# Rounding the expert activation to its high part: all 96 on ScalarE instead of 28 there and 68 on VectorE

## The chip, the cores and the metric

The kernel runs on one core of a Trainium2 chip. The metric is the device time of one execution in microseconds (us). TensorE (PE, with its weight loads PEld), VectorE (DVE), ScalarE (ACT), GpSimd (POOL) and SyncE (SP, which issues most DMAs) each work through their own queue in order and wait for one another through semaphores. "The granted clock" is the share of TensorE's full clock that the throttle let through.

## The reference

Three stages follow each other: a chunked linear attention with decay, a dense feed-forward layer with the activation h * cos(h), and a mixture of 8 experts with top-1 gating and a capacity. The change touches the second.

```python
def _attn_ref(x, a, B, C):               # 4 x 8 heads, 768 tokens, 24 chunks of 32
    ...
        L = np.exp(cum[:, :, :, None] - cum[:, :, None, :]) * causal
        M = np.einsum('bhin,bhjn->bhij', Cc, Bc) * L
        y[:, :, sl] = M @ xc + (Cc @ state) * decay_to_i
        state = decay_full * state + sum_j(B_j x_j decay_from_j)
    ...
def _moe_ref(x, w_in, w_out):            # x: 3072 x 256, w_in: 256 x 2048
    h = x @ w_in
    g = h * np.cos(h)
    return (g @ w_out).astype(np.float32)

def _moe2_ref(x, w_gate, w1, w2, capacity):   # 8 experts, 256 -> 1024 -> 256
    expert_idx = np.argmax(x @ w_gate, axis=1)
    ...
    h = np.maximum(np.einsum('ecd,edf->ecf', disp, w1), 0.0)
    y = np.einsum('ecf,efd->ecd', h, w2)
    out[i] = gate_w[i] * y[expert_idx[i], pos[i]]
```

## The kernel before

**Precision.** Matmul operands are split into a high part (fp32r) and the remainder that the rounding left. A product is three matmuls: high with high, low weight with high activation, high weight with low activation.

**The dense layer's loop.** The 3072 tokens are 6 tiles `t` of 512, the 2048 hidden units 16 blocks `f` of 128: 96 iterations `it = 16 t + f`, counted from 0. One iteration is

- `mm1` (L919, PE): six matmuls into a PSUM bank `hp` (three buffers);
- `c_round` (L926, ACT): adds a large constant, which rounds h in turns to an integer, into `g` (three buffers); reads `hp`;
- `c_frac` (L930, DVE): the difference, from `g` and `hp`;
- `c_sin` (L933, ACT): the cosine as a shifted sine, in place in `g`; ACT reloads its function table before it where an exponential ran last;
- `c_mul` (L936, DVE): h times the cosine, from `hp` and `g`; with it `hp` comes free;
- `c_hi` (L945 on ACT or L947 on DVE): copies `g` to `gh`, rounded to fp32r (three buffers). This is the operation of the change;
- `c_lo` (L952, POOL): `gl = g - gh` (three buffers);
- `mm2` (L964, PE): six matmuls, four with `gh` and two with `gl`, into the two banks `yt` of the tile.

**Order.** Every piece of work is put into a list with a position, mostly the iteration number plus an offset from the table `OFF`, and the list is sorted by position and emitted. That is the order in each engine's queue. For one iteration `it` of tiles 1 to 4 the positions are: `mm1` +0, `c_round` +0.059, `c_frac` +0.438, `c_sin` +1.002, `c_mul` +1.165, `c_hi` +1.474, `c_lo` +2.061, `mm2` +4.08. In the steady state ACT's queue therefore has `c_sin(it-1)`, `c_round(it)` and, where it is on ACT, `c_hi(it-1)`, then `c_sin(it)`; DVE's has `c_mul(it-1)`, `c_frac(it)` and, where it is on DVE, `c_hi(it-1)`. The positions do not depend on the engine that `c_hi` runs on.

**What runs between.** The attention of later token groups is put between the iterations, one group of 256 tokens every 8. Of it matter here: `a_diff` (L670), a 128 x 2048 addition in SBUF, on POOL for all groups but one; `a_mask` (L661, POOL); the exponential (L680, ACT, with a table load); `a_m` (L789, DVE), which multiplies the scores in PSUM (`sp`, from L781 on PE) by the decay; `a_y` (L835, L839, PE), which needs L789's result; `a_st` (L814, L817, L818, DVE), the state, of which L818 has two operands in SBUF; `a_evh` (L848, ACT) and `a_evl` (L854, DVE), which take `yp` from PSUM into the next tile's operand `xT`. Also between them: the splitting of the dense layer's weights in iterations 0 to 15 (L879, L884, L889 on DVE, L901 on ACT, L905 mostly on POOL), the splitting of the first experts' weights (L1225 on ACT, L1246 mostly on POOL, L1250 on DVE), and the routing of each finished tile (L972 to L1105). From about 446 us on the experts' loop runs (L1538 to L1659).

**Which engine rounds.** Before, `c_hi` runs on ACT for `3 <= it < 16` and `79 <= it < 94`, that is 28 times, and on DVE for the other 68:

```python
    GHA = [[3, 16], [79, 94]]
    gh_act = lambda it: any(a <= it < b for a, b in GHA)
```

Of the kernel before, what the change touches and what calls it, by code (L numbers as in the profile page):

```python
# [374 lines left out]
def fused_kernel(ctx: ExitStack, tc: tile.TileContext, I, out: bass.AP):  # L375
# [559 lines left out]
    def c_mul(it):  # L935
        nc.vector.tensor_tensor(GT[it], HP.pop(it), GT[it], op=ALU.mult)  # L936

    GHA = [[3, 16], [79, 94]]
    gh_act = lambda it: any(a <= it < b for a, b in GHA)

    def c_hi(it):
# [860 lines left out]
```

## Time and profile before

| | us |
|---|---|
| Median of 3 runs (lowest, highest) | 643.16 (642.65, 646.45) |
| Profiled execution, whole | 644.14 |
| Its span, first to last instruction | 642.4 |
| Mean granted TensorE clock | 0.932 |
| `c_hi` on DVE (L947), 68 times, busy | 56.8 |
| `c_hi` on ACT (L945), 28 times, busy | 17.5 |

How to read the lines that follow: a group of instructions is given by line, engine, operation and tiles, with its count, busy time, the mean of one in ns, the engine's idle time just before it, and what ended that. The row of one line has the shortest, median and longest duration in ns. A wait has the waiting instruction, the releasing one, the total in us, how often, and the longest. A timeline row has start and duration in us, and in brackets the idle time of the engine before it. A row of the windows view has start and end, length, busy time and count for each engine, the granted clock, the DMA share and GB/s. [...]

### The profile page before, as it was taken

Reading aid. Unit: us, or ns where it says so; the run is one execution under the profiler, and the core shown is the slowest. Engines: PE = TensorE matmul, PEld = TensorE weight load, DVE = VectorE, ACT = ScalarE, POOL = GpSimd, SP = SyncE. Lnnn points to the kernel's source line nnn. Section 1 sums busy time; section 2 is a strip of 40 time slices with the busy share of each in tenths; the row PEclk is TensorE's granted clock in tenths of the full one; section 3 lists DMA queues with packets and bytes.
Section 4 is the critical chain, followed back from the end, with each engine's and each line's share of the span. In section 5 each row is a group of like instructions: output and inputs, shape, how many; then the busy total and the mean of one; then the engine's idle time right before and its main releaser. Section 6 shows DMA issues by size and latency. Waiting matters only on the chain. (4 is left out here: it accounts for less than half of the span.)

```text
span 642.4 us, 9919 instructions
## 1 busy us (share of the span) xinstructions
PE 546.6 (85%) x2860; PEld 381.8 (59%) x2860; DVE 524.4 (82%) x1009; ACT 336.9 (52%) x601; POOL 388.3 (60%) x409
## 2 busy tenths in 40 slices
PE   8848869998979897997989989685766799999993
PEld 7426647786767676785768777463433445555552
DVE  7989998779998999889987988988696885555663
ACT  5446677574547545473647658564735553333220
POOL 6889877766476756576665344478537563542343
PEclk9876898898999999898989999897978999999998
DMA  7799534250705162434431222045589989995772
GB/s 244 207 319 337 156 115 148 99 181 15 230 34 191 56 212 68 148 99 139 141 117 49 79 86 98 34 115 153 112 199 251 246 167 186 168 173 118 141 155 72
DMA packets 128021, 94.07 MB, mean 146 GB/s; under 512 B 81918, under 2 KB 116800, under 8 KB 127968
## 3 DMA queue, kind: packets, MB, share of 16 engines
q1 hardware_dynamic: 125184, 86.46, 50.2%
q0 software_dynamic: 2784, 6.97, 4.1%
q8 instruction: 26, 0.43, 0.3%
q14 instruction: 27, 0.22, 0.1%
HBM read 59.50 MB, written 15.54 MB: 117 GB/s over the span
## 5 line engine op out<-in xcount | busy, mean ns | idle before, releaser
L952 POOL TENSOR_TENSOR gl<-g,gh 128x512 fp32r<-128x512 f32 x96 | 131.5, 1370 | 82.2 <-DVE gh L947 54.6
L919 PE MATMUL hp<-xT,w_in 128*128 128x512 f32 x576 | 163.8, 424 | 6.6 <-DVE g L936 6.6
L919 PEld LDWEIGHTS hp<-xT,w_in 128*128 128x128 f32 x576 | 111.3, 202 | 32.1 <-DVE g L936 8.0
L964 PE MATMUL yt<-gh,w_out 128*128 128x512 f32 x384 | 109.8, 406 | 6.6 <-DVE gh L947 6.6
L933 ACT ACTIVATE g<-g,halfpi 128x512 f32<-128x512 f32 x96 | 69.2, 720 | 67.4 <-DVE g L930 65.0
L964 PEld LDWEIGHTS yt<-gh,w_out 128*128 128x128 f32 x384 | 75.7, 198 | 24.4 <-DVE gh L947 7.0
L1612 ACT ACTIVATE hr<-hp 128x512 f16<-128x512 f32 x58 | 34.5, 595 | 79.7 <-PE hp L1606 64.8
L936 DVE TENSOR_TENSOR g<-hp,g 128x512 f32<-128x512 f32 x96 | 65.6, 684 | 12.9 <-ACT g L933 12.5
L930 DVE SCALAR_TENSOR_TENSOR g<-g,hp 128x512 f32<-128x512 f32 x96 | 65.1, 678 | 10.0 <-ACT g L926 10.0
L1616 DVE SCALAR_TENSOR_TENSOR hr<-hp,hr 128x512 f16<-128x512 f32 x58 | 40.0, 689 | 34.8 <-ACT hr L1612 31.8
L964 PE MATMUL yt<-gl,w_out 128*128 128x512 f32 x192 | 61.9, 399 | 7.4 <-POOL gl L952 7.4
L926 ACT ACTIVATE g<-hp 128x512 f32<-128x512 f32 x96 | 56.0, 583 | 13.5 <-PE hp L919 11.6
L947 DVE TENSOR_SCALAR gh<-g 128x512 fp32r<-128x512 f32 x68 | 56.8, 836 | 0.0
L1631 PE MATMUL yp<-w2a,ht 128*128 x116 | 42.4, 402 | 15.1 <-DMA ht<-hr 8.2
L1631 PEld LDWEIGHTS <-ht 128*128 128x128 f16 x232 | 23.1, 100 | 44.4 <-DMA ht<-hr 16.9
L1643 POOL TENSOR_TENSOR sc<-gall,invb 128x1 f32<-128x1 f32 x58 | 13.1, 225 | 56.8 <-DVE yacc L1654 47.0
L1538 POOL DMA_INDIRECT xr<-xs_d,gat x29 | 36.0, 1240 | 18.3 <-DVE ob L1120 4.6
L964 PEld LDWEIGHTS yt<-gl,w_out 128*128 128x128 f32 x192 | 36.2, 192 | 17.9 <-POOL gl L952 10.3
L1631 PE MATMUL yp<-w2b,ht 128*128 x116 | 39.0, 379 | 0.0
L1659 POOL DMA_INDIRECT out_dram<-yacc,scat x29 | 29.0, 999 | 14.2 <-issue 14.2
L848 ACT ACTIVATE xT<-yp 128x256 fp32r<-128x256 f32 x24 | 9.2, 384 | 49.2 <-PE yp L839 49.1
L1606 PEld LDWEIGHTS <-xkeep 128*128 128x128 f16 x192 | 19.5, 104 | 25.2 <-issue 8.2
(239 smaller groups left out, 1126.0 us busy)
## 6 DMA issues: line engine op xcount, KB each, us to landing
wst<-in_w_dram SPq DMA_DIRECT2D x32, 512.0 KB
ex<-cumc_d SPq DMA_DIRECT2D x10, 1024.0 KB
pre<-in_w_io_dram SPq DMA_DIRECT2D x14, 512.0 KB
hl_d<-hl SPq DMA_DIRECT2D x10, 512.0 KB
b<-hl_d SPq DMA_DIRECT2D x40, 128.0 KB
c4s<-hl_d SPq DMA_DIRECT2D x40, 128.0 KB
xb<-in_xB_dram SPq DMA_DIRECT2D x11, 384.0 KB
xs_d<-xs SPq DMA_DIRECT2D x6, 514.0 KB
```

The source lines that it names most:

```text
L919: nc.tensor.matmul(hp, w_in[:, f, wl, k, :], xT[:, k, xl, :], start=(n == 0), stop=(n == 5))
L926: nc.scalar.activation(g, HP[it], AF.Copy, bias=MAGIC + 0.25)
L930: nc.vector.scalar_tensor_tensor(g, g, MAGIC, HP[it], op0=ALU.subtract, op1=ALU.subtract)
L933: nc.scalar.activation(GT[it], GT[it], AF.Sin, scale=SIN_SCALE, bias=halfpi)
L936: nc.vector.tensor_tensor(GT[it], HP.pop(it), GT[it], op=ALU.mult)
L947: nc.vector.tensor_scalar(gh, GT[it], 1.0, None, op0=ALU.mult)
L952: nc.gpsimd.tensor_tensor(gl, GT.pop(it), GH[it].bitcast(F32), op=ALU.subtract)
L964: nc.tensor.matmul(YT[t][k], w_out[:, f, wl, k * P:(k + 1) * P], g, start=(f == 0 and j == 0), stop=(f == NF - 1 and j == 2))
L1538: nc.gpsimd.indirect_dma_start(out=xr, out_offset=None, in_=xs_d, in_offset=bass.IndirectOffsetOnAxis(ap=gat[k][:, n:n + 1].bitcast(U32), ...
L1612: nc.scalar.activation(hr[:, 0], HPB[j], AF.Relu)
L1616: nc.vector.scalar_tensor_tensor(hr[:, 1], HPB.pop(j), 0.0, hr[:, 0], op0=ALU.max, op1=ALU.subtract)
L1631: nc.tensor.matmul(yp.rearrange("p a b -> p (a b)"), ht[:, k, :], w[:, bass.ds(e, 1), k].rearrange("p a l b -> p (a l b)"), start=(k == 0) ...
```

## The change

The list of ranges in which the rounding runs on ACT becomes one range over all 96 iterations. So `c_hi` always takes its first branch (L945), and the 68 VectorE instructions of L947 become ScalarE activations with the function Copy. Nothing else is edited: the positions, the buffers and the other engines' instructions stay.

```diff
@@ -935,7 +935,7 @@
     def c_mul(it):
         nc.vector.tensor_tensor(GT[it], HP.pop(it), GT[it], op=ALU.mult)
 
-    GHA = [[3, 16], [79, 94]]
+    GHA = [[0, 96]]
     gh_act = lambda it: any(a <= it < b for a, b in GHA)
 
     def c_hi(it):
```

## The prediction

> **What bounds the kernel now.** I read the page's totals first, then busy time by stage (the windows view), the costliest groups, the waits, and last the timeline around the longest wait.
>
> ```profile
> PE 546.6 (85%) x2860; PEld 381.8 (59%) x2860; DVE 524.4 (82%) x1009; ACT 336.9 (52%) x601; POOL 388.3 (60%) x409
> 36.00:62.00 26.00, 14.37 (x41) 10.39 (x40) 23.52 (x26) 13.71 (x20) 25.08 (x18) 0.61 0.99 330
> 115.00:381.00 266.00, 239.47 (x1275) 189.30 (x1274) 239.51 (x472) 151.08 (x251) 162.93 (x131) 0.96 0.34 112
> 381.00:446.00 65.00, 49.88 (x235) 38.37 (x234) 56.91 (x125) 43.96 (x78) 41.28 (x40) 0.92 0.34 101
> 446.00:642.00 196.00, 166.80 (x885) 87.71 (x884) 127.24 (x269) 73.57 (x138) 92.98 (x148) 0.95 0.81 165
> ```
>
> The columns after the length are busy time of PE, PEld, DVE, ACT and POOL, the granted clock, the DMA share and GB/s. Iterations 16 to 78 of the first expert stage, whose rounding is now on DVE, fill the stretch from 115 to 381 us. There PE and DVE are each busy for 239.5 of 266 us, and ACT has 115 us free. So in this stage PE and DVE share the bound, and the question is what of DVE's time makes PE wait.
>
> ```profile
> L952 POOL TENSOR_TENSOR gl<-g,gh 128x512 fp32r<-128x512 f32 x96 | 131.5, 1370 | 82.2 <-DVE gh L947 54.6
> L947 DVE TENSOR_SCALAR gh<-g 128x512 fp32r<-128x512 f32 x68 | 56.8, 836 | 0.0
> ...
> L947 DVE TENSOR_SCALAR gh<-g x68: 411/422/3632, 42.9 to 444.6; 128x512 fp32r<-128x512 f32 x68
> L945 ACT ACTIVATE gh<-g x28: 614/624/635, 62.7 to 436.0; 128x512 fp32r<-128x512 f32 x28
> ```
>
> The moved group has a median of 0.422 us, yet a mean of 0.836: 68 x 0.422 = 28.7 of its 56.8 us are work, and the other 28.1 are stalls. The longest takes 3.632, and the timeline shows why:
>
> ```profile
> 217.69 0.68 DVE L930 SCALAR_TENSOR_TENSOR g<-g,hp 128x512 f32<-128x512 f32 x1
> 218.00 3.62 POOL L670 TENSOR_TENSOR ex<-ex,ncum 128x2048 f32<-128x2048 f32 x1
> 218.28 3.63 DVE L947 TENSOR_SCALAR gh<-g 128x512 fp32r<-128x512 f32 x1
> 218.40 0.72 ACT L933 ACTIVATE g<-g,halfpi 128x512 f32<-128x512 f32 x1 [0.40 <-DVE g L930]
> 219.03 0.58 ACT L926 ACTIVATE g<-hp 128x512 f32<-128x512 f32 x1
> 221.83 0.68 DVE L789 TENSOR_TENSOR ex<-sp,ex 128x512 f32<-128x512 f32 x1
> 222.43 0.68 DVE L936 TENSOR_TENSOR g<-hp,g 128x512 f32<-128x512 f32 x1
> 222.56 0.49 PE L835 MATMUL yp<-bct,st 128*128 128x128 f32 x2 [2.59 <-DVE ex L789]
> 223.03 0.41 DVE L817 TENSOR_TENSOR tmp<-up,hmask 128x256 f32<-128x256 f32 x1
> 223.47 0.48 DVE L818 SCALAR_TENSOR_TENSOR st<-st,ex,tmp 128x256 f32<-128x256 f32 x1
> 224.11 2.87 PE L919 MATMUL hp<-xT,w_in 128*128 128x512 f32 x6
> ```
>
> The rounding starts on DVE 0.28 us after POOL's L670 and ends with it. L789, queued right behind, comes 3.2 us late, and PE, whose next work needs its result, stands 2.59 us. This happens seven times, once in each later pass of L670. The first and the last on DVE and on PE are
>
> ```profile
> 119.45 3.37 DVE L947 TENSOR_SCALAR gh<-g 128x512 fp32r<-128x512 f32 x1
> 320.43 3.63 DVE L947 TENSOR_SCALAR gh<-g 128x512 fp32r<-128x512 f32 x1
> ...
> 123.47 0.49 PE L835 MATMUL yp<-bct,st 128*128 128x128 f32 x2 [1.28 <-DVE ex L789]
> 324.72 0.49 PE L835 MATMUL yp<-bct,st 128*128 128x128 f32 x2 [2.26 <-DVE ex L789]
> ...
> PE yp L835 <- DVE ex L789: 11.1, 6, 2.6
> PE yp L839 <- DVE ex L789: 8.5, 6, 2.6
> PE hp L919 <- DVE g L936: 6.2, 4, 1.9
> ```
>
> and the seven PE waits (1.28, 2.59, 2.34, 2.59, 2.22, 2.65, 2.26) sum to 15.9 us of the 25.8 that PE waits for DVE in this stretch (the last three rows). A wait also costs afterwards:
>
> ```profile
> 224.00:228.00 4.00, 4.00 (x18) 3.11 (x11) 3.96 (x7) 1.70 (x3) 1.74 (x2) 0.57 0.41 139
> 210.44 1.52 PE L919 MATMUL hp<-xT,w_in 128*128 128x512 f32 x6
> ```
>
> Right behind the wait at 222 us the granted clock is 0.57 for 4 us, and six matmuls take 2.87 us against 1.52 at 210 us. Over the 266 us the mean clock of 0.96 is a loss of 266 x 0.04 = 10.6 us of matmul time.
>
> **The change part by part.**
>
> (a) The seven waits. L947 leaves DVE's queue, so L789 follows L930 at once and has its operand (PE's `sp` was done). I take all 15.9 us off; the bounds are 0 and 15.9.
>
> (b) The slow clock behind them. Bounds 0 and 10.6. Part of a slow spell lies beside DVE's catching up. ACT's waits for the first matmul group in this stretch (L926 below, 9.3 us in 9) are the part that reaches the activation chain; most follow these spells. I take 7.
>
> ```profile
> ACT g L933 <- DVE g L930: 52.1, 40, 4.2
> ACT g L926 <- PE hp L919: 9.3, 9, 1.7
> ```
>
> [...]
>
> (c) The other 61 roundings free 61 x 0.42 = 25.6 us of DVE. Most lies beside PE's work. PE's remaining waits for DVE are 25.8 - 15.9 = 9.9 us (bounds 0 and 9.9); DVE loses about a tenth of its load, so I take 2.
>
> (d) The first three roundings, at 42.9, 48.7 and 57.4 us, took 0.94 to 0.95 each on DVE against 0.62 on ACT; POOL and DVE are both near full in 36 to 62 us, so I take 0.5 (bounds -2 to 2). The last two cost 0.2 us more each, at most 0.4 in all, taken as nothing: DVE's other work behind them covers it.
>
> (e) What ACT pays: 68 x 0.624 = 42.4 us. In its queue the rounding of an iteration stands behind the next iteration's L926 and ahead of its L933. L933 waits for L930, which stands behind L936 on DVE; the rounding needs only L936. So 0.62 us on ACT falls into the 0.68 us in which DVE does L930, inside the 52.1 us that ACT now waits there (row above). Neither form issues a DMA. Where the cover is gone: behind an exponential, ACT itself is late and reloads its table,
>
> ```profile
> 208.37 0.58 ACT L926 ACTIVATE g<-hp 128x512 f32<-128x512 f32 x1
> 208.97 1.28 ACT L933 ACT_TABLE_LOAD   x1
> 210.27 0.72 ACT L933 ACTIVATE g<-g,halfpi 128x512 f32<-128x512 f32 x1
> ```
>
> and the rounding goes between the first two rows. At most 7 x 0.62 = 4.4 us; PE is busy there, so I take 2. What queues behind a rounding that waits for L936 is L848 (PE's `yp` to `xT`), the routing copies and L933; POOL's L952 and then PE's L964 wait for its result, placed some 2.6 iterations later.
>
> (f) The stall may pass on. L789, L936 and L817 read `sp`, `hp` and `up` from PSUM, and no row of these shows a stall; L818, two SBUF operands, comes 0.60 + 0.60 + 0.44 = 1.6 us after the rounding's old place, when POOL's L670 has up to 1.6 us to go. That it can be held is shown where the rounding already is on ACT:
>
> ```profile
> 89.07 3.82 POOL L670 TENSOR_TENSOR ex<-ex,ncum 128x2048 f32<-128x2048 f32 x1
> 89.33 4.11 DVE L889 SCALAR_TENSOR_TENSOR wcv<-wst,wcv 128x512 int32<-128x512 int32 x1
> ```
>
> Seven times 1.3 us is 9 us on DVE (bounds 0 to 11). PE by then has `yp` and two matmul groups to do, so I take 3. [...]
>
> Sum: -15.9 - 7 - 2 - 0.5 + 2 + 3 = -20.4. The profiled execution took 644.14 us (span 642.4), 0.98 above the median of 643.16; 644.14 - 20.4 - 0.98 is 622.8, so **623 us**. Stages behind 446 us start earlier and keep their length: their waits are on each other and on transfers that they issue.
>
> **The rivals.**
> [...]
> - *The stall is handed on and PE stands again*: if L818, or the next two-operand instruction, makes the following L789 late by what (a) gained, only (c) and (d) are left: 643.2 - 2.5 = 641 us, no measurable change. For it: L889 at 89 us. Against: L789 and L936 are ahead of L818.
> - *ACT becomes the bound*: one mechanism, L933 pushed back by the rounding ahead of it in every iteration. ACT has 151 + 61 x 0.62 = 189 of 266 us, so it must come from order, not load. If all 0.624 lands on the path, 68 x 0.624 = 42.4 against 25.4 gained by (a) to (d): 643.2 + 17 = 660. It turns slower than before at 25.4 / 68 = 0.37 us an iteration. For it: in 381 to 446 us ACT's roundings waited 12.8 us for L936, in 7 of 15.
>
> ```profile
> ACT gh L945 <- DVE g L936: 12.8, 7, 5.4
> ```
>
>   Against: behind that wait L933 would have waited for L930 anyway.
> - *PE runs closed up*: all of (a), (b) and (c) at their ends, nothing paid: 643.2 - 36.4 = 607.
>
> **How the numbers follow.** Forecast 0.50, dips stay 0.16, closed up 0.08, handed on 0.15, ACT the bound 0.11. The likeliest alone spans 615 to 632. For 8 in 10 the range is 609 to 641: it takes in the first two, most of "closed up" and about half of "handed on". Within 1% (6.4 us) is about what a measurement of this kernel can tell from no change. Faster by over 1%: 0.50 + 0.16 + 0.08 = 0.74; within 1%: 0.15; slower: 0.11.
>
> **What would show it.** L945 x96 at about 0.62 us and no L947; no DVE instruction of 3.6 us right ahead of an L789; PE's waits for L789 down from 19.6 us to under 6; the clock of this stage above 0.97 and the stage near 246 us; L818 up to about 1.8 us under L670; ACT's waits for L930 down by some 30 us, with new waits of L945 for L936. The forecast is wrong if PE's waits for L936 grow past 20 us (ACT's order), if L789 is still late, or if the stage shortens and the part behind it lengthens.

## The result, and the profile after

The median of the changed kernel is 629.17 us (4 runs, 628.82 to 630.46) against 644.31 us for the kernel before beside it: a ratio of 0.9757 (95% interval 0.9721 to 0.9792), 15.1 us less. The profiled execution took 629.44 us (span 627.7, mean granted clock 0.947) against 644.14 (642.4, 0.932). The prediction was 623 us, 609 to 641.

First the page's totals and the groups of the rounding and its neighbours, after:

```profile
PE 538.4 (86%) x2860; PEld 376.1 (60%) x2860; DVE 482.7 (77%) x941; ACT 372.0 (59%) x669; POOL 391.5 (62%) x409
...
L945 ACT ACTIVATE gh<-g 128x512 fp32r<-128x512 f32 x96 | 60.2, 627 | 61.3 <-DVE g L936 54.6
L936 DVE TENSOR_TENSOR g<-hp,g 128x512 f32<-128x512 f32 x96 | 65.8, 685 | 33.4 <-ACT g L933 33.2
```

VectorE has 68 instructions and 41.7 us less, ScalarE 68 more and 35.1 us more (the totals count time in which records overlap once). The last row has changed: VectorE now waits 33.2 us for the cosine L933 before L936, against 12.5 us before.

The windows view of after, by the same stages as before:

```profile
36.00:62.00 26.00, 14.53 (x47) 10.42 (x46) 24.89 (x28) 16.98 (x27) 22.55 (x19) 0.74 1.02 338
112.00:366.00 254.00, 235.92 (x1283) 186.89 (x1282) 198.32 (x409) 184.97 (x317) 167.95 (x134) 0.97 0.37 121
366.00:431.00 65.00, 51.21 (x234) 39.53 (x233) 56.52 (x123) 45.57 (x82) 40.25 (x39) 0.89 0.31 93
431.00:628.00 197.00, 165.31 (x885) 87.07 (x884) 126.86 (x269) 73.31 (x138) 94.20 (x148) 0.96 0.81 165
```

The stage from 115 to 381 us took 266 us and takes 254; the two behind it keep their length (65 and 196 to 197). To compare more exactly I take as "the stretch" the time from the start of L926 of iteration 16 to that of iteration 79, which lie here on ScalarE's timeline, before and then after:

```profile
116.04 0.58 ACT L926 ACTIVATE g<-hp 128x512 f32<-128x512 f32 x1
375.86 0.58 ACT L926 ACTIVATE g<-hp 128x512 f32<-128x512 f32 x1
```

```profile
114.92 0.58 ACT L926 ACTIVATE g<-hp 128x512 f32<-128x512 f32 x1
359.80 0.58 ACT L926 ACTIVATE g<-hp 128x512 f32<-128x512 f32 x1
```

The stretch goes from 259.8 to 244.9 us, 14.9 less, and the profiled executions differ by 14.7. So the whole gain is made in these 63 iterations; what lies ahead gives 1.1 us and what lies behind takes 1.3.

What became of the seven stalls? This is the timeline of after at the pass of L670 that the prediction showed:

```profile
211.42 0.68 DVE L930 SCALAR_TENSOR_TENSOR g<-g,hp 128x512 f32<-128x512 f32 x1
211.54 3.63 POOL L670 TENSOR_TENSOR ex<-ex,ncum 128x2048 f32<-128x2048 f32 x1
211.60 0.64 ACT L945 ACTIVATE gh<-g 128x512 fp32r<-128x512 f32 x1 [0.33 <-DVE g L936]
212.02 0.69 DVE L789 TENSOR_TENSOR ex<-sp,ex 128x512 f32<-128x512 f32 x1
212.14 0.62 ACT L584 ACTIVATE hl<-bct 128x512 fp32r<-128x512 f32 x1
212.66 0.71 ACT L933 ACTIVATE g<-g,halfpi 128x512 f32<-128x512 f32 x1
213.40 0.69 DVE L936 TENSOR_TENSOR g<-hp,g 128x512 f32<-128x512 f32 x1 [0.70 <-ACT g L933]
214.00 0.41 DVE L817 TENSOR_TENSOR tmp<-up,hmask 128x256 f32<-128x256 f32 x1
214.45 0.99 DVE L818 SCALAR_TENSOR_TENSOR st<-st,ex,tmp 128x256 f32<-128x256 f32 x1
```

L789 follows L930 at once, as predicted (it starts at 212.02, 0.08 us ahead of the end of L930's record). Two smaller payments show in the same rows. L818 takes 0.99 instead of 0.48 us and ends 0.27 us behind L670: part of the hold is handed on. And VectorE stands 0.70 us before L936, because the rounding (211.60 to 212.24) and a copy behind it put L933 after the end of L930 (212.10).

The waits of after in 112 to 366 us, PE's, then ScalarE's:

```profile
PE yp L839 <- DVE ex L789: 5.6, 4, 2.3
PE hp L919 <- DVE g L936: 4.9, 5, 1.9
PE yp L835 <- DVE ex L789: 3.9, 2, 2.6
...
ACT gh L945 <- DVE g L936: 40.7, 42, 5.2
ACT g L933 <- DVE g L930: 10.2, 7, 3.2
```

PE still waits 9.5 us for L789, in six waits, two behind the gating of each of three tiles. The timeline of after shows one of them, some 10 us behind the pass above:

```profile
220.04 2.02 POOL L661 TENSOR_SCALAR_AFFINE_SELECT ex<-ex 128x2048 f32<-128x2048 f32 x1
220.17 1.94 DVE L1054 TENSOR_TENSOR rsm<-rsm,desc 128x32 f32<-128x32 f32 x1
222.47 0.68 DVE L789 TENSOR_TENSOR ex<-sp,ex 128x512 f32<-128x512 f32 x1
223.21 0.49 PE L835 MATMUL yp<-bct,st 128*128 128x128 f32 x2 [1.30 <-DVE ex L789]
```

L1054, a tiny instruction of the gating (L1051 to L1056, both operands in SBUF), lasts 1.94 us and ends with POOL's L661; L789 is queued behind it, and PE waits. It is the same pattern with another held instruction. The gating was held like this before as well, with two PE waits of 1.3 us behind it.

Last, how VectorE spends the stretch, by its row of the windows view and its longest wait there. Before:

```profile
116.00:376.00 260.00, 235.29 (x1257) 186.12 (x1256) 234.73 (x463) 146.36 (x244) 159.37 (x128) 0.95 0.34 111
...
DVE g L936 <- ACT g L933: 5.7, 12, 1.0
```

After:

```profile
115.00:360.00 245.00, 228.78 (x1259) 181.38 (x1258) 193.88 (x403) 178.60 (x306) 162.82 (x129) 0.98 0.36 117
...
DVE g L936 <- ACT g L933: 23.5, 32, 3.1
```

VectorE's busy time falls by 234.7 - 193.9 = 40.8 us, and its idle time rises from 25.3 to 51.1 us, by 25.8; the difference is the 15 us gained. Of the 25.8, 17.8 us are the wait for L933 (5.7 to 23.5). PE's idle time fell by only 8.5 us (24.7 to 16.2), and its busy time by 6.5 with the higher clock. Such a sum closes for every engine; it says where the time went, not which engine set the pace.

### The profile page after: what moved, and what is told of

It is laid out like the page before. It is cut to its first block, busy times and chain, and to the rows that moved or that the text cites. A ratio compares the mean times of both kernels' runs of the same rounds, so it can differ in the third digit from the quotient of the medians.

```text
span 627.7 us, 9931 instructions
## 1 busy us (share of the span) xinstructions
PE 538.4 (86%) x2860; PEld 376.1 (60%) x2860; DVE 482.7 (77%) x941; ACT 372.0 (59%) x669; POOL 391.5 (62%) x409
## 5 line engine op out<-in xcount | busy, mean ns | idle before, releaser
L952 POOL TENSOR_TENSOR gl<-g,gh 128x512 fp32r<-128x512 f32 x96 | 136.1, 1421 | 67.5 <-ACT gh L945 38.4
L919 PE MATMUL hp<-xT,w_in 128*128 128x512 f32 x576 | 162.0, 419 | 5.7 <-DVE g L936 4.9
L919 PEld LDWEIGHTS hp<-xT,w_in 128*128 128x128 f32 x576 | 110.0, 200 | 31.3 <-DVE g L936 6.3
L964 PE MATMUL yt<-gh,w_out 128*128 128x512 f32 x384 | 109.1, 404 | 6.1 <-ACT gh L945 6.1
L945 ACT ACTIVATE gh<-g 128x512 fp32r<-128x512 f32 x96 | 60.2, 627 | 61.3 <-DVE g L936 54.6
L936 DVE TENSOR_TENSOR g<-hp,g 128x512 f32<-128x512 f32 x96 | 65.8, 685 | 33.4 <-ACT g L933 33.2
L964 PEld LDWEIGHTS yt<-gh,w_out 128*128 128x128 f32 x384 | 75.1, 197 | 23.6 <-ACT gh L945 6.6
L933 ACT ACTIVATE g<-g,halfpi 128x512 f32<-128x512 f32 x96 | 68.9, 718 | 18.9 <-DVE g L930 18.6
L930 DVE SCALAR_TENSOR_TENSOR g<-g,hp 128x512 f32<-128x512 f32 x96 | 65.0, 677 | 12.7 <-ACT g L926 12.6
L964 PE MATMUL yt<-gl,w_out 128*128 128x512 f32 x192 | 62.1, 400 | 6.8 <-POOL gl L952 6.8
L926 ACT ACTIVATE g<-hp 128x512 f32<-128x512 f32 x96 | 55.9, 582 | 8.5 <-PE hp L919 5.6
L1631 PE MATMUL yp<-w2a,ht 128*128 x116 | 41.5, 395 | 15.5 <-DMA ht<-hr 7.2
L964 PEld LDWEIGHTS yt<-gl,w_out 128*128 128x128 f32 x192 | 36.0, 190 | 17.1 <-POOL gl L952 9.6
L1654 DVE SCALAR_TENSOR_TENSOR yacc<-yp,sc,yacc 128x256 f32<-128x256 f32 x58 | 27.9, 481 | 8.0 <-ACT yacc L1648 3.7
```

What stands on the lines that cost most here:

```text
L919: nc.tensor.matmul(hp, w_in[:, f, wl, k, :], xT[:, k, xl, :], start=(n == 0), stop=(n == 5))
L926: nc.scalar.activation(g, HP[it], AF.Copy, bias=MAGIC + 0.25)
L930: nc.vector.scalar_tensor_tensor(g, g, MAGIC, HP[it], op0=ALU.subtract, op1=ALU.subtract)
L933: nc.scalar.activation(GT[it], GT[it], AF.Sin, scale=SIN_SCALE, bias=halfpi)
L945: nc.scalar.activation(gh, GT[it], AF.Copy)
L952: nc.gpsimd.tensor_tensor(gl, GT.pop(it), GH[it].bitcast(F32), op=ALU.subtract)
```

## The experiments

Three questions were open: are the seven stalls the gain, what holds L789 after them, and what does ScalarE's side cost? Each kernel below is the kernel before or after with one edit. In the table the ratio is against the kernel before on the same chip; stretch, VectorE's busy and idle time in it are from one profile each, the changes against before's 259.8 us, so no interval stands behind them.

| kernel | median | ratio (95%) | stretch | change | busy | idle |
|---|---|---|---|---|---|---|
| before | 644.3 | | 259.8 | | 234.5 | 25.3 |
| after, all 68 | 629.17 | 0.9757 (0.9721 to 0.9792) | 244.9 | -14.9 | 193.7 | 51.2 |
| seven alone | 642.04 | 0.9934 (0.9902 to 0.9967) | 254.2 | -5.6 | 223.5 | 30.7 |
| other 61 alone | 642.68 | 0.9961 (0.9924 to 0.9998) | 253.5 | -6.3 | 207.3 | 46.2 |
| seven late on VectorE | 652.08 | 1.0106 (1.0072 to 1.0140) | 262.6 | +2.8 | 234.8 | 27.8 |
| after, cosine first | 632.62 | 0.9806 (0.9760 to 0.9853) | 245.2 | -14.6 | 191.6 | 53.6 |
| after, gating later | 622.16 | 0.9651 (0.9604 to 0.9699) | 235.6 | -24.2 | 188.9 | 46.7 |
| before, filler at the wait | 651.52 | 1.0069 (1.0028 to 1.0110) | 262.8 | +3.0 | 228.9 | 33.9 |
| seven and gating later | 633.63 | 0.9834 (0.9792 to 0.9876) | 246.5 | -13.3 | 219.9 | 26.6 |
| before, gating later | 642.02 | 0.9950 (0.9926 to 0.9973) | 255.2 | -4.6 | 229.3 | 25.9 |
| 32 of the 68 | 640.43 | 0.9927 (0.9900 to 0.9955) | 251.6 | -8.2 | 208.4 | 43.2 |
| before, filler ahead | 653.03 | 1.0141 (1.0092 to 1.0190) | 259.3 | -0.5 | 234.5 | 24.8 |
| gating and positions later | 626.80 | 0.9708 (0.9659 to 0.9757) | 239.2 | -20.6 | 187.9 | 51.4 |
| after, rounding twice | 658.40 | 1.0216 (1.0171 to 1.0262) | 269.7 | +9.9 | 190.3 | 79.4 |

The part from the start of L926 of iteration 95 to the end, in which no edit moves more than the last two roundings, took 203.0 us before, 202.8 after and 203.9 to 208.7 in the other profiles. So these profiled executions hold some 1 to 6 us that lie behind the edited part. Whether the other executions of the same kernels do is not known, so both columns are read.

**The seven alone, and the other 61 alone.** The seven roundings that stand under L670 go to ScalarE in the kernel before; then, in the kernel after, these seven go back to VectorE.

```diff
-    GHA = [[3, 16], [79, 94]]
+    GHA = [[3, 17], [79, 94]] + [[k, k + 1] for k in range(24, 65, 8)]
```

> The kernel before with only seven more roundings on ScalarE, those of iterations 16, 24, 32, 40, 48, 56 and 64, which stood 3.4 to 3.6 us behind GpSimd's L670; the other 61 stay on VectorE. Theory A (the gain is the seven stalls): nearly the whole gain of the change, 12 to 16 us below the kernel before, ratio 0.975 to 0.982, and no VectorE instruction of 3.6 us ahead of L789 in these seven places. Rival B (the gain is VectorE's lighter load, spread over the 68): seven of 68 parts, 1 to 3 us, ratio 0.995 to 0.999.

```diff
-    GHA = [[0, 96]]
+    GHA = [[0, 16], [65, 96]] + [[k + 1, k + 8] for k in range(16, 64, 8)]
```

> The changed kernel with the same seven roundings put back on VectorE: 61 of the 68 moved. Theory A: the seven stalls and PE's seven waits of 1.3 to 2.7 us behind them are back, and the time is within 4 us of the kernel before, ratio 0.993 to 1.005. Rival B: nine tenths of the gain, ratio near 0.978.

By the ratio the seven alone give 0.0066 x 645 = 4.3 us, the 61 alone 2.5; by the stretch 5.6 and 6.3. So neither is the gain: the theory that the seven stalls carry nearly all of it falls, although the seven alone has no stall of 3.4 to 3.6 us left (three other roundings are held for 2.0 to 2.3 us). The rival, nine tenths for the 61, falls too: their median stays in the range of the first theory. By the ratios the two parts give 6.8 us of the 15.7 of all 68, so each gives more beside the other than alone. The timeline of the seven alone shows the next hold, at the gating again,

```profile
160.19 2.03 POOL L661 TENSOR_SCALAR_AFFINE_SELECT ex<-ex 128x2048 f32<-128x2048 f32 x1
160.54 1.72 DVE L1056 TENSOR_TENSOR oh_all<-rsm 128x32 bf16<-128x32 f32 x1
162.19 0.68 DVE L789 TENSOR_TENSOR ex<-sp,ex 128x512 f32<-128x512 f32 x1
162.92 0.64 PE L839 MATMUL yp<-ex,xb 128*32 128x128 f32 x4 [3.59 <-DVE ex L789]
```

and its waits of PE for L789 in the stretch are still 12.1 us:

```profile
PE yp L839 <- DVE ex L789: 8.1, 5, 3.6
PE yp L835 <- DVE ex L789: 4.0, 3, 1.8
```

The other 61 alone keep the stall (here the same pass):

```profile
214.72 3.43 DVE L947 TENSOR_SCALAR gh<-g 128x512 fp32r<-128x512 f32 x1
...
218.81 0.49 PE L835 MATMUL yp<-bct,st 128*128 128x128 f32 x2 [2.77 <-DVE ex L789]
```

and yet its stretch is shorter. In the stretch, relief of VectorE that leaves these PE waits for L789 in place is worth as much as the removal of the stalls; by the ratios, whose intervals overlap, it can't be ordered.

**The seven later on VectorE.** In the kernel before the seven stay on VectorE, but behind L789 and the next L936 in its queue.

```diff
-        put('gh', it, c_hi, it, t=t)
-        put('gl', it, c_lo, it, t=t)
+        if it in range(16, 65, 8):
+            put('ghx', it + 2.18, c_hi, it)
+            put('glx', it + 2.19, c_lo, it)
+        else:
+            put('gh', it, c_hi, it, t=t)
+            put('gl', it, c_lo, it, t=t)
```

> The kernel before, all 68 roundings still on VectorE, with those seven placed two instructions later in its queue, behind L789 and L936 (L952 of these iterations right behind them on GpSimd). VectorE's instructions and load are unchanged and ScalarE gets nothing. Theory A, sharpened (what cost is not the stall but that L789 stood behind it): PE's seven waits for L789 vanish though each rounding is still held, now for 1.5 to 2.5 us; 8 to 15 us below before, ratio 0.977 to 0.988. Rival B: no change, 0.998 to 1.002. If moving the stall later only moves PE's wait to the next L789: within 3 us of before.

It became slower (stretch +2.8), although PE's seven waits did vanish as expected. In the pass of L670 that starts at 150.01 us L835 now follows without a wait, and the rounding is held behind it:

```profile
151.20 0.39 PE L835 MATMUL yp<-bct,st 128*128 128x128 f32 x2
151.77 2.15 DVE L947 TENSOR_SCALAR gh<-g 128x512 fp32r<-128x512 f32 x1
```

The waits of PE for L789 that the stretch still has stand behind the gating, as with the seven alone. The longest, then the sums:

```profile
163.20 0.64 PE L839 MATMUL yp<-ex,xb 128*32 128x128 f32 x4 [4.28 <-DVE ex L789]
...
PE yp L839 <- DVE ex L789: 9.0, 5, 4.3
PE sp L781 <- DVE xT L854: 6.1, 5, 1.8
```

PE now waits 6.1 us for L854 as well. VectorE's busy time is that of before (234.8 against 234.5). So PE's seven waits can go without any gain while VectorE's work and holds stay. (L952 of these iterations moved with the rounding; part of the 2.8 us may be that.)

**The cosine ahead of the rounding.** In the kernel after, the rounding's position goes from 1.4743 to 2.03, behind the next L933 in ScalarE's queue.

```diff
- 'gh': 1.4743,
+ 'gh': 2.03,
```

> The changed kernel with the rounding of tiles 1 to 4 placed behind the next iteration's L933 in ScalarE's queue (position +2.03 instead of +1.474). In the changed kernel VectorE waits 25.4 us for L933 in the stretch from 112 to 366 us, 33 times, as the rounding stands ahead of it. Theory C (this wait is the price of the change and lies on the path): the wait falls below 10 us and the time falls 2 to 6 us below the changed kernel, to 623 to 627. Rival D (VectorE has room for it): the wait falls, the time stays within 1.5 us of 629. If the later rounding holds GpSimd's L952 and then PE's L964: slower than 631.

VectorE's waits in the stretch:

```profile
DVE g L930 <- ACT g L926: 16.2, 30, 2.8
DVE g L936 <- ACT g L933: 15.9, 32, 1.4
```

The wait for L933 falls from 23.5 to 15.9 us, but that for L926 rises from 8.9 to 16.2, and the stretch is the same (245.2). In the stretch, the rounding's place in ScalarE's queue chooses which wait shows, and the cost stays. The profile is of the fastest of five executions; the median, 632.62 us, lies in the range that the expectation gave to a late L952. But GpSimd's waits for L945 rose only from 32.4 to 35.4 us, and PE waits nowhere in the stretch for L952, so that cause is not shown.

**The gating later.** In the kernel after, the first gating piece (L1051 to L1056) is put 1.1 iterations later, behind the L789 that it held up.

```diff
- 'rg1': 10.746,
+ 'rg1': 11.87,
```

> The changed kernel with the gating of tiles 0 to 3 (L1051 to L1056, which GpSimd's L661 holds for 1.2 to 2 us each) placed behind the two products L789 that PE waits for, not ahead of them (position 11.87 instead of 10.746). In the changed kernel PE waits 2.33 + 1.38, 1.30 + 0.96 and 2.57 + 0.96 us for L789 right behind them, 9.5 us in all. Theory E (these waits are what became late next, and took back part of the gain): they vanish and the time falls 5 to 10 us, to 619 to 624. Rival: PE waits for L1056 ahead of L1066 or for L936 instead, and the time stays within 2 us of 629.

This is the fastest kernel: 622.16 us, with an interval of the ratio below that of after. PE waits nowhere in its stretch for L789; its longest wait is

```profile
PE pp L1066 <- DVE oh_all L1056: 4.7, 3, 2.0
```

Then the same edit with only the seven moved, and in the kernel before alone:

> The seven roundings alone on ScalarE, as in the run with only those seven, and the gating (L1051 to L1056) of tiles 0 to 3 behind the two products L789, as in the run with the late gating. With the seven alone the time fell by 4 us only: PE's seven waits were gone, and waits of 3.59 + 1.49, 1.79 + 1.30 and 1.84 + 1.09 us stood behind the gating instead. Theory H (the gating ahead of L789 is what took the rest): these go too, 630 to 635, ratio 0.975 to 0.984. Theory J (VectorE's queue paces: with the seven alone it is still busy for 223 of 254 us, as in turn L818, L1250, L947 and the gating are held; PE only waits elsewhere): within 3 us of the seven alone, 637 to 642.

> The kernel before with the late gating alone; all 68 roundings stay on VectorE where they were. Theory H: PE's two waits of 1.3 us behind the gating go and the seven stay, 2 to 4 us gained. Theory J: VectorE's queue is no shorter, within 2 us of before, ratio 0.997 to 1.003.

In the kernel before, the later gating alone takes 4.6 us off the stretch (3.2 by the ratio); with the seven moved the two take 13.3 (10.7), with all 68 moved 24.2 (22.6). The windows row of the seven with the gating later:

```profile
115.00:361.00 246.00, 228.42 (x1255) 180.25 (x1254) 219.56 (x452) 148.37 (x250) 162.06 (x128) 0.98 0.36 118
```

It is almost as short as after with 26 us more of VectorE's time: seven roundings moved and one piece of gating shifted come close to 68 moved. PE's waits for L789 that the seven left behind (8.1 and 4.0 us) are gone in it but for 0.9 us. In the kernel before, with the stalls kept, this row of PE's waits stays:

```profile
PE yp L835 <- DVE ex L789: 11.3, 6, 2.6
```

In the stretch, moving the seven or the gating is worth some 5 us each, both together 13: the one exposes the other.

**The positions later too.** The next two routing pieces also go later.

```diff
- 'rg1': 10.746,
+ 'rg1': 11.87,
- 'rp1': 12.78,
+ 'rp1': 13.72,
- 'rp2': 13.756,
+ 'rp2': 14.3,
```

> The changed kernel with the late gating, and with what follows from the gating later too: the matmuls of the positions (L1066, L1069) at 13.72 instead of 12.78, and VectorE's part behind them (L1077 on) at 14.3 instead of 13.756, for tiles 0 to 3. With the late gating alone PE waits 1.85, 0.80 and 2.01 us for L1056 ahead of L1066. Theory: PE's next wait again stands where VectorE's held gating ends; moved behind it, 2 to 5 us are gained on 622, so 617 to 620. Rival (VectorE paces now): within 1.5 us of 622. It also tells whether the version with the late gating is near the best of these.

The expected gain did not come: it is slower than with the gating alone by 3.6 us of stretch, and by 4.6 us in the medians; PE's longest wait there is now another:

```profile
PE hp L919 <- DVE g L936: 10.2, 4, 3.7
```

**Half of the 68.** Every second rounding from iteration 16 to 78 goes to ScalarE, the seven among them.

```diff
-    GHA = [[3, 16], [79, 94]]
+    GHA = [[3, 17], [79, 94]] + [[k, k + 1] for k in range(18, 79, 2)]
```

> The kernel before with 32 of the 68 moved: the even iterations from 16 to 78, the seven among them; the gating stays ahead of L789. Theory J (what VectorE sheds beyond the seven is worth time until PE paces): between the seven alone and all 68, 633 to 637, ratio 0.981 to 0.988. Theory H (the gating's waits are all that is left): as with the seven alone, 639 to 643.

The stretch falls by 8.2 us, between the seven alone (5.6) and all (14.9); the median, 640.43, is that of the seven alone within the intervals. Its windows row:

```profile
117.00:369.00 252.00, 231.31 (x1259) 181.69 (x1258) 208.95 (x433) 162.27 (x275) 160.72 (x129) 0.97 0.36 115
```

VectorE has 26 us less work and 18 us more idle time. By the stretch there is a dose beyond the seven, by the ratios it can't be told; the median lies in the range of the theory that names the gating's waits alone.

**The clock behind the waits.** Filler matmuls should keep PE busy in the kernel before, first in front of L835, then in front of L781.

```diff
+        if g >= 5 and c == 0:
+            for _ in range(8):
+                nc.tensor.matmul(yp[:, 0, :], ones_f, ones_f, start=True, stop=True)
```

> The kernel before with eight more matmuls of 128x128 constants on PE ahead of the first L835 or L839 of each group from the sixth on; they write a bank that the next matmul overwrites, and change nothing that is computed. They fall into PE's seven waits of 1.3 to 2.7 us and take 1.5 to 3.5 us each time. Theory F (the wait itself lowers the clock behind it, so filling it is a gain): the clock of the stretch from 115 to 381 us rises from 0.96 to 0.98 or more, and the time is 1 to 6 us below the kernel before. Rival G (the dips come in any case): the clock stays at 0.96, and the time rises by what the filling is longer than the waits, 0 to 8 us.

```diff
-        for u in range(2):
+        for u in [0, 1] * (5 if g >= 5 and c == 0 and q == 1 else 1):
```

> The kernel before with the score matmuls L781 that precede PE's seven waits done five times over (the same values again, eight more matmuls of 128x256, about 1.7 us, inside waits of 1.3 to 2.7 us; the earlier filler stood behind the wait, as its bank came free only with L789). Nothing that is computed changes. Theory F (a wait of PE of over 2 us lowers the clock behind it): the slow spells behind the seven waits go, the clock of the stretch from 115 to 381 us rises from 0.96 to about 0.99, and the time falls by 1 to 5 us. Rival G (the spells are no path: VectorE paces): the clock rises, the time stays within 2 us. Rival G2: the clock stays.

The first told nothing on its question: its bank came free only with L789, so the filler ran behind the wait and was load. The clock of its stretch rose to 0.98 all the same, and the stretch became 3.0 us longer.

```profile
153.64 2.68 PE L835 MATMUL yp<-ones_f 128*128 128x128 f32 x13 [2.60 <-DVE ex L789]
```

The second ran ahead of it; one of the filled groups, the wait behind it, and the stretch:

```profile
148.65 1.53 PE L781 MATMUL sp<-c4s,b 128*128 128x256 f32 x10
154.81 0.49 PE L835 MATMUL yp<-bct,st 128*128 128x128 f32 x2 [1.65 <-DVE ex L789]
...
115.00:374.00 259.00, 235.35 (x1310) 187.96 (x1309) 234.38 (x462) 146.30 (x242) 159.76 (x128) 0.98 0.35 112
```

PE did some 56 matmuls more, its seven waits shrank from 15.9 to 11.0 us, and the clock of the stretch rose from 0.95 to 0.98. The stretch stayed as it was (259.3 against 259.8), with VectorE's busy time unchanged. So in the kernel before the slow clock did not set the pace of the stretch. The 2 us of Theory F was the author's guess, and no run shows such a border: in the kernel before, the clock was 0.66 from 123.9 to 127.9 us, behind the wait of 1.28 us, and 1.00 from 191 to 195 us, behind that of 2.34 us. On the waits themselves this run says nothing: a filled wait ends, like an empty one, when L789 ends (L835 starts 0.05 us behind it here at 154.81 us, and in the kernel before at 222.56 us). That they can go without a gain is what the seven later on VectorE show. Nor is PE without part in the pace: in the chain of work that ended last, followed back through it, L919 and L964 hold 15.5 and 12.3% of this run's stretch. The median is 1.4% longer. The profiled execution is the fastest of four (648.12 to 656.87); in it the part from iteration 95 on is 5.7 us longer than before, and the cause is open.

**The rounding twice.** In the kernel after, ScalarE does each rounding of iterations 16 to 78 twice.

```diff
-            nc.scalar.activation(gh, GT[it], AF.Copy)
+            for _ in range(2 if 16 <= it < 79 else 1):
+                nc.scalar.activation(gh, GT[it], AF.Copy)
```

> The changed kernel with each ScalarE rounding of iterations 16 to 78 done twice (the same values into the same buffer): 63 more activations of 0.63 us, 39.5 us of ScalarE, nothing else. It measures what ScalarE's place is worth. If a rounding there lies fully beside other work (term (e) of the prediction): within 3 us of the changed kernel's 629. If ScalarE is at its limit in this stretch (the rival in which it becomes the bound): a rise of 25 to 40 us. In between, the rise divided by 63 is the price of 0.63 us on ScalarE per iteration, to be set against 0.37 us from which the change would have lost.

Its stretch and the longest wait of VectorE in it:

```profile
116.00:386.00 270.00, 236.98 (x1255) 184.32 (x1254) 190.84 (x404) 215.60 (x367) 162.66 (x129) 0.96 0.33 108
...
DVE g L936 <- ACT g L933: 41.9, 36, 3.8
```

Against the kernel after, the 63 extra copies of 0.63 us cost 24.8 us of stretch, 0.39 each, and 29.2 us by the medians, 0.46 each. More than half of a further ScalarE copy in an iteration comes through to the end, though ScalarE is busy for only 216 of 270 us.

## Why the prediction was right, step by step

The side and the range were right. The sum was 5 to 6 us too hopeful (-20.4 against -14.7 between the profiled executions), and single terms were further off and partly cancelled, so that it came this near is in part luck.

- **What bounds the stretch.** "PE and DVE share the bound" was half right. Removing PE's seven waits with VectorE's work left as it was (the seven later) and raising the clock (the filler ahead) gained nothing in the stretch, while the 61 roundings taken off VectorE gained with PE's waits left in place. The runs point to VectorE's in-order queue, in a ring with ScalarE and PE, as what sets the pace; the question the prediction then put, which of VectorE's time makes PE wait, was too narrow. No run added work to VectorE alone, so that it sets the pace is argued from these runs and not measured directly.
- **(a) -15.9, the seven waits: mis-sized.** The mechanism was right: the stalls were there, are gone, and L789 follows L930 at once. Alone they are worth 4.3 us by the ratio and 5.6 in the stretch. What fails is the step "I take all 15.9 us off": PE's wait is no measure of the gain (the seven later take the same waits away and gain nothing), and the gating under L661 held L789 next. With the gating moved too, both give 13.3.
- **(b) -7, the slow clock: mis-sized.** The clock rose (0.96 to 0.97 over the stage, 0.95 to 0.98 over the stretch), and PE's busy time in the stretch fell by 6.5 us, close to the 7. But the filler ahead raised the clock to the same 0.98 for no time, so nothing shows that the term is a gain. Without the term the sum is 623 + 7 = 630 us, next to the result, and nothing is also what the filler gives for the clock; but dips that stay, which the prediction gave 0.16, are not what happened, as the clock did rise. That the result lies so near 630 is luck.
- **(c) -2, the other 61: too small.** Alone they give 2.5 us by the ratio and 6.3 in the stretch; on top of the seven, 14.9 - 5.6 = 9.3 in the stretch. The 25.6 us of relief were costed only against PE's remaining waits, not against VectorE's own queue. The count was off as well: the stretch has 63 of the 68 roundings, so 56 of the 61 lie in it, 23.5 us, and the other five are those that (d) counts again.
- **(d) -0.5, the first three.** Iteration 16 starts 1.1 us earlier than before, within the bounds. But the kernels with the first three roundings still on VectorE start it anywhere from 114.7 to 116.9 us, and after has 114.9, so no run here shows this term.
- **(e) +2, what ScalarE pays: too small.** ScalarE's wait for L930 fell by 42 us (52.1 to 10.2), as much as the price in busy time, as the cover promised. But the cover is not free: L945 stands 40.7 us waiting for L936, and VectorE's wait for L933 rose by 17.8 us. "The rounding falls into the 0.68 us of L930" did not hold in the pass shown above, where a copy stood between it and L933. The doubled rounding puts the marginal price at 0.39 to 0.46 us; that a further copy costs so much doesn't say what the first one did.
- **(f) +3, the stall handed on: right in kind, incomplete.** L818 was held under L670 in five of the seven passes, for 0.98 to 1.28 us instead of 0.48: 2.8 us of VectorE in all, against the 9 of the prediction. The larger payment was not L818's but the gating's, which no step named.
- **The rivals.** "Handed on" was partly there: 9.5 us of PE's waits for L789 stayed, where the prediction wanted under 6. "ACT becomes the bound" had the right mechanism, VectorE's waits for L933, and these waits grew by 17.8 / 63 = 0.28 us an iteration. That is below its turning point of 0.37, though that point rests on the 25.4 us of (a) to (d), which the runs do not bear out term by term. With the doubled rounding this rival decides: 658.40 us. That this lies near its 660 is chance, as it is another kernel.

In these rows a held VectorE instruction lasts until GpSimd's ends: L947 at 3.63 us and L818 at 0.99 under L670, and L1054 at 1.94 under L661, end within 0.3 us of them. These three have all operands in SBUF; L789, with one operand in PSUM, runs its 0.69 us beside L670. That the place of the operands is what decides was not shown, as no run moves an operand.

What stays open: how much of the 9.3 us beyond the seven is relief of VectorE's queue and how much is the gating's hold meeting less behind it, why the two parts give so much less alone than together by the ratios, and why the parts from iteration 95 on differ by up to 5.9 us between profiles.

## What to carry to other kernels

Before a wait is counted as a gain, ask of each engine that is nearly full what the edit does to its busy time and what to its idle time: here 40.8 us less work on VectorE came with 25.8 us more idle time. Filling a wait with work does not test what the wait costs, as it ends no earlier; moving its cause does. When a held instruction leaves a queue, look for the next instruction with the same weakness ahead of the same consumer; moving both was worth 13 us of the stretch where each alone was worth some 5. An engine with a quarter of its time free can still pass on most of an instruction added to it: here ScalarE, busy for 178.6 of 245 us, waiting for VectorE and waited for by it, passed on 0.39 of 0.63 us, some 60%.

## What was not expected of the hardware

- Some waits of PE were followed by a slow clock: in the kernel before, the granted clock was 0.57 from 224 to 228 us, behind a wait of 2.59 us. From 191 to 195 us, behind a wait of 2.34 us, it was 1.00, so it does not follow every time. With more work for PE, ahead of such waits (filler ahead) or behind them (filler at the wait), the mean clock of the stretch was 0.98 instead of 0.95.
- The holds of VectorE went by what POOL had left to do, not by the instruction's own size: in the kernel after, the gating's instruction of 128 x 32 elements (L1054) lasted 1.94 us beside an affine select of 2.02 us, and 0.19 us at its shortest; in the kernel before, L947 lasted 3.63 us beside L670's 3.62, against a median of 0.42.
